# When the second quarter of w_in, the second stage's matrix and the first conversion come in a spectral MLP kernel's start

## The chip, the cores and the metric

The kernel runs on one core of a Trainium2 chip. The metric is the device time of one execution in microseconds (us), the median of several executions. TensorE (PE) multiplies matrices, with weight loads shown apart as PEld; VectorE (DVE) and ScalarE (ACT) do element-wise work; SyncE (SP) and ScalarE issue the DMA transfers that matter here.

## The reference

The input x is (8, 3008, 256). Each batch goes through a real FFT along its 3008 rows, a complex linear map with a soft threshold, and an inverse FFT; the rows that come out go through a two-layer network with a leaky ReLU. Cut to what is computed:

```python
X = np.fft.rfft(x, axis=1)
Yr = Xr @ w_r - Xi @ w_i + b_r
Yi = Xr @ w_i + Xi @ w_r + b_i
Yr = np.sign(Yr) * np.maximum(np.abs(Yr) - 0.01, 0.0)   # Yi alike
y = np.fft.irfft(Y, n=3008, axis=1)
h = y @ w_in                       # 256 -> 2048
out = np.maximum(0.01 * h, h) @ w_out   # 2048 -> 256
```

w_in and w_out arrive as 64-bit floats, which the kernel reads as pairs of 32-bit words and converts itself.

## The kernel before, in words

3008 is 47 x 64, so each FFT is done in two stages of small matrix products. For one batch b:

- `fwd(b)` is the first stage (47 points). It loads x in seven column chunks of two halves (L237 for batch 0), forms sums and differences of the halves on DVE (`fold`, L247 and L248), multiplies each of the 14 results by a matrix in fa (`stage_a`, L264; the bank tag `psh` has four buffers), copies the product back to SBUF on ACT (L266) and stores it to `u_dram` (L269, issued on SP for batch 0). The list `turned` holds the copy, `written` the stores.
- `mid(b)` is the second stage (64 points) with the linear map. For each of 12 pairs j of frequencies it reads `u_dram` back with two loads in another order (L331, kept in `reads`, three `u` buffers), multiplies by slices of fb (`stage_b`, L345), evicts on ACT (L349) and DVE (L350), multiplies by the weights (`proj`, L80), adds the bias (L382), thresholds (L390 to L392), scales (L396, L400), and multiplies by gb (`stage_g`). The result is copied (L418) and stored to `v_dram` by ACT (L420). Pair j uses index 0 of fb and the two indices 2j+1 and 2j+2, out of 25.
- `inverse` and `forms` do the last 47-point stage and make token chunks of 512 columns; `moe` runs the two-layer network on 47 such chunks (L94 for w_in, L609 for w_out).

Turning the first spectrum means that all 14 stores of batch 0 have to land before the first read of `mid(0)`, since the reads cut across every chunk.

Around this the start of the program does the constants. `load_win(c)` loads quarter c of w_in in two transfers of 512 KB each (L157); quarters 0 and 1 share a buffer tile, as do 2 and 3. `convert_win(c)` turns it from 64-bit floats into a high and a low 32-bit part: two operations on ACT (L133, L134), five on DVE (L135 to L139), one sum (L164), four small combinations (L167 to L170) and three splits (L173 on ACT, L174 on DVE). `split_consts` does the same splitting for the other constants (L114 on ACT, L115 on DVE).

The order of work on each engine is set by a planner that simulates the program (`schedule_with_timeline_sim=True`, L867). The code steers it with `tc.issue_after(ins)`: what is traced inside such a block is put behind `ins` on the engine of `ins`, and left free on the other engines. Data dependences come on top by themselves. Before the change these were the hints at the start: the second quarter's loads on SP behind the eighth store (`written[7]`), `convert_win(0)` without a hint, `split_consts` and `convert_win(1)` on ACT behind the last of the 14 copies (`turned` held only the last), the bias, quarters 2 and 3 and ga on SP behind the fourth read (`reads[3]`).

The main loop alternates `moe_a`, `moe_b` and `moe_o` of successive chunks on PE in a fixed order, with the spectra of later batches laid in between.

Of the kernel before, what the change touches and what calls it, by code (L numbers as in the profile page):

```python
# [8 lines left out]
F32 = mybir.dt.float32  # L9
# [9 lines left out]
N1, N2, NK1 = 47, 64, 24  # L19
NG, NS = 5, 13  # L20
P = 128
# [9 lines left out]
def spectral_mlp_kernel(  # L31
# [33 lines left out]
    const = ctx.enter_context(tc.tile_pool(name="const", bufs=1))  # L65
# [3 lines left out]
    sync, act, dve, pool = nc.sync, nc.scalar, nc.vector, nc.gpsimd  # L69

    def bank(tag, bufs):
        return ps.tile([P, 512], F32, name=tag, tag=tag, bufs=bufs)

    def products(dst, pairs):

        terms = []
        for l, r in pairs:
            terms += [(l[0], r[0]), (l[0], r[1]), (l[1], r[0])] if len(l) == 2 else [(l[0], r[0])]
        for i, (a, b) in enumerate(terms):
            last = nc.tensor.matmul(dst, a, b, start=(i == 0), stop=(i == len(terms) - 1))  # L80
        return last
# [18 lines left out]
    consts = {}  # L100

    def pair(name, shape):
        consts[name] = tuple(const.tile(shape, F32R, name=f"{name}_{p}") for p in ("hi", "lo"))
        return consts[name]

    def load_plain(name, src, shape):
        consts[name] = const.tile(shape, F32, name=name)
        sync.dma_start(consts[name], src)
# [19 lines left out]
    def float64_parts(raw, a, q):  # L128


        wl, wh = raw[:, :, 0], raw[:, :, 1]
        u = a.bitcast(U32)
        act.mul(q, wl, 2.0 ** -52)  # L133
        act.activation(a, wh.bitcast(F32), AF.Abs, scale=2.0 ** 16)  # L134
        dve.tensor_scalar(a, a, F64_MIN * 2.0 ** 16, F64_MAX * 2.0 ** 16, ALU.max, ALU.min)  # L135
        dve.tensor_scalar(u, u, 4, 1, ALU.logical_shift_left, ALU.logical_shift_right)
        dve.scalar_tensor_tensor(u, wh, 0x80000000, u, ALU.bitwise_and, ALU.bitwise_or)
        dve.tensor_scalar(wl, u, 0xFF800000, None, ALU.bitwise_and)
        dve.tensor_mul(q, q, wl.bitcast(F32))  # L139
# [8 lines left out]
    def load_win(c, queues, behind=None):  # L148
        if c % 2 == 0:
            tag = ("wout_hi", "wout_lo")[c // 2]  # L150
            raw = sb.tile([P, 2, NH * NIN, 2], U32, name="win_raw", tag=tag, bufs=1)
            win_raw.extend((raw[:, 0], raw[:, 1]))
        r = win_raw[c].rearrange("p (a f) w -> p a (f w)", a=NH)
        iv = w_in.bitcast(U32).rearrange("(a p) f -> p a f", p=P)[:, :, 2 * c * NIN:2 * (c + 1) * NIN]
        for a, q in enumerate(queues):
            with tc.issue_after(behind.ins) if behind is not None else nullcontext():
                q.dma_start(r[:, a], iv[:, a])  # L157

    def convert_win(c):


        a, q, s = win_tmp
        float64_parts(win_raw[c], a, q)
        dve.tensor_add(a, a, q)  # L164
        a = a.rearrange("p (j q i m) -> p j q i m", j=NH, q=2, i=2)
        a11, a12, a21, a22 = (a[:, j, :, i] for i in range(2) for j in range(2))
        dve.tensor_add(s[:, 0], a21, a22)  # L167
        dve.tensor_sub(s[:, 2], a11, a21)
        dve.tensor_sub(s[:, 1], s[:, 0], a11)
        dve.tensor_sub(s[:, 3], a12, s[:, 1])  # L170
        hi, lo = (w[:, :, 2 * c:2 * c + 2] for w in consts["win"])
        for k, w in ((slice(0, 2), a[:, :, :, 0]), (2, a22), (slice(3, 7), s)):
            act.copy(hi[:, k], w)  # L173
            last = dve.tensor_sub(lo[:, k], w, hi[:, k].bitcast(F32))  # L174
        return last
# [37 lines left out]
    reads, written, turned, turning, thresholded = [], [], [], [], []  # L213
# [4 lines left out]
    def fwd(b):  # L218
        ud = dram.tile([2, NK1, NG * NS, D], F32, name="u_dram", tag="u_dram", bufs=NPRE + 1)
        u_dram[b] = ud  # L220
        uv = ud.rearrange("c k (g s) d -> c (k g) (s d)", g=NG)
        x_t, s_t = {}, {}

        def load(c):
            cols = slice(2 * c * D, min(2 * c + 2, NS) * D)
            n = cols.stop - cols.start
            if b < NPRE:
                tag, bufs = (XT, XT1)[b][c]
                x2 = sb.tile([PA, 2, 2 * D], F32, name="xin", tag=tag, bufs=bufs)
                x_t[c] = [x2[:, h, :n] for h in range(2)]  # L230
            else:
                x_t[c] = [
                    sb.tile([PA, 2 * D], F32, name=f"xin{h}", tag="uv"[h], bufs=3 - h)[:, :n] for h in range(2)
                ]
            for h, t in enumerate(x_t[c]):
                if b == 0:
                    (act if h else sync).dma_start(t, x[b, h, :, cols])  # L237
                else:
                    with tc.issue_after(reads[-1].ins):
                        sync.dma_start(t, x[b, h, :, cols])  # L240

        def fold(c):
            xa, xb = x_t[c]
            n = xa.shape[1]
            eng = dve
            xs = sb.tile([PA, 2 * D], F32, name="xs", tag="zf", bufs=1)[:, :n] if b else xs3[:, c % 3, :n]
            eng.tensor_add(xs, xa, xb)  # L247
            eng.tensor_sub(xa, xa, xb)  # L248
            s_t[c] = [(xs,), (xa,)] if b < NPRE else [xs, xa]

        def split(c, h):
            t = s_t[c][h]
            n = t.shape[1]
            z = sb.tile([PA, 2, 2 * D], F32R, name="xz", tag="ez"[h], bufs=1)
            xh, xl = z[:, 0, :n], z[:, 1, :n]
            dve.tensor_copy(xh, t)
            dve.tensor_sub(xl, t, xh.bitcast(F32))  # L257
            s_t[c][h] = (xh, xl)

        def stage_a(c, h):  # L260
            t = x_t[c][h]
            n = t.shape[1]
            pa = (bank("psf", 2) if b else bank("psh", 4))[:PA, :n]
            products(pa, [(consts[f"fa{h}"] if b else consts[f"fa{h}32"], s_t[c][h])])  # L264
            t = x_t[c][1 - h]
            cp = act.copy(t, pa)  # L266
            if b == 0:
                turned[:] = [cp]
            st = (act if b else sync).dma_start(uv[h, :, 2 * c * D:2 * c * D + n], t)  # L269
            if b == 0:  # L270
                written.append(st)

        def stage_a1(c):

            n = x_t[c][0].shape[1]
            pas = [(bank("psf", 2) if c in (4, 5) else bank("psh", 4))[:PA, :n] for _ in range(2)]
            for h in range(2):
                with tc.issue_after(turning[NPAIR - 2].ins):
                    products(pas[h], [
                        (consts[f"fa{h}32"], (x_t[c][0],)), (consts[f"fa{2 * h}32"], (x_t[c][1],))])  # L280
            for h in range(2):
                act.copy(x_t[c][h], pas[h])
                sync.dma_start(uv[h, :, 2 * c * D:2 * c * D + n], x_t[c][h])

        if b == 1:
            for c in range(NX):
                load(c)
                yield 0
            for c in (0, 1, 2, 3, 6, 4, 5):
                stage_a1(c)  # L290
                yield 6 * x_t[c][0].shape[1]
            return

        ahead = 2 if b >= NPRE else NX
        for c in range(ahead):
            load(c)
        yield 4 * CS if b >= NPRE else 0
        fold(0)
        if b >= NPRE:
            split(0, 0)  # L300
        yield 0
        for c in range(NX):
            for h in range(2):
                if h == 0 and c + ahead < NX:
                    load(c + ahead)
                if h == 0 and c + 1 < NX:
                    fold(c + 1)
                stage_a(c, h)
                if b >= NPRE and (c + h < NX):
                    split(c + h, 1 - h)  # L310
                yield 3 * x_t[c][h].shape[1]
# [381 lines left out]
    f0 = Stream(fwd(0), FWD)  # L693
    f0.to(0.01)
    load_win(0, (sync, act))
    load_plain("fb", fb, [P, NK1 + 1, N2])
    load_weights()
    sign = const.tile([P, NK1 + NPAIR], F32, name="sign")
    sync.dma_start(sign, sg)
    sync.dma_start(consts["gb32"][0], gb)  # L700
    f0.finish()
    load_win(1, (sync, sync), written[7])
    pair("win", [P, 7, NQ, P])
    win_tmp = (
        sb.tile([P, NH * NIN], F32, name="cva", tag="vin"), sb.tile([P, NH * NIN], F32, name="cvq", tag="gf"),
        sb.tile([P, 4, 2, P], F32, name="ws", tag="yh"))
    act.mul(fa32[:, 2], fa32[:, 1], -1.0)
    convert_win(0)
    with tc.issue_after(turned[0].ins):
        split_consts()  # L710
    m0 = Stream(mid(0), MID)
    m0.to(0.001)
    bias = const.tile([P, 2, D], F32, name="bias")
    with tc.issue_after(reads[3].ins):
        for r, src in enumerate((b_r, b_i)):
# [3 lines left out]
    with tc.issue_after(reads[3].ins):  # L719
        load_plain("ga", ga, [PA, 2, P])  # L720
    fp = Stream(fwd(1), FWD)
    with tc.issue_after(turned[0].ins):
        convert_win(1)
    wout = load_wout()
    for i in range(1, 17):
# [147 lines left out]
```

## Time and profile before

| | us |
|---|---|
| median of 3 runs | 2574.14 |
| the three runs | 2566.14, 2574.14, 2575.76 |
| the profiled execution | 2568.88 |
| its span, from first to last instruction | 2567.10 |
| PE busy in the span | 2527.2 (98%) |
| DVE busy | 1882.8 (73%) |
| ACT busy | 1677.5 (65%) |

The profiled execution took 1.78 us more than its span. It lies between the shortest and the other two runs. In the timeline, each row gives the start in us, the time in us, the engine, the line in the kernel, the operation, what it writes and reads and how many instructions are merged in the row; in brackets stands how long the engine was idle before, and what it waited for. SPq and ACTq rows are the issuing of DMA transfers, not the transfers themselves. In the table by stages, the columns are the length of the stage, the busy us of each engine with its instructions in brackets, the granted TensorE clock (1 is full speed), the busy share of the 16 DMA engines, and the GB/s that they moved.

### The profile page before, as it was taken

The numbers are of one execution on the slowest core, as the hardware profiler recorded it, in microseconds if no ns is written. First come the engines' busy times: TensorE is split into PE (matmuls) and PEld (weight loads), VectorE is DVE, ScalarE is ACT, GpSimd is POOL, SyncE is SP. The second block draws the span as 40 slices with busy tenths as digits, with TensorE's granted clock in tenths as the row PEclk, the third lists the DMA queues.
The fourth block names the chain that finished last, engine by engine and source line by source line (L and its number), as shares of the span: only waits on it lengthen the run. The fifth ranks groups of instructions, "written<-read, shape, count | busy, mean of one in ns | idle before, by whom it ended". The sixth has DMA issues, their size and how long they took to land.

```text
span 2567.1 us, 42449 instructions
## 1 busy us (share of the span) xinstructions
PE 2527.2 (98%) x16204; PEld 2269.8 (88%) x16204; DVE 1882.8 (73%) x3460; ACT 1677.5 (65%) x3151; POOL 118.9 (5%) x96
## 2 busy tenths in 40 slices
PE   6999999999999999999999999999999999999999
PEld 4689888999899998999989999899998998999998
DVE  7787777777877778777787677867768777666665
ACT  4776666677566765677666676567665676655564
POOL 0001000000000000000000000000000000000000
PEclk8999999999999999999999999999999999999999
DMA  8631133111321113111141111412114111100000
GB/s 267 176 93 50 42 91 88 41 50 45 103 67 46 50 37 112 59 49 49 42 113 53 50 49 38 120 54 58 34 38 132 46 54 41 44 21 29 9 17 17
DMA packets 119904, 165.12 MB, mean 64 GB/s; under 512 B 13597, under 2 KB 69909, under 8 KB 119701
## 3 DMA queue, kind: packets, MB, share of 16 engines
q1 hardware_dynamic: 79112, 115.54, 14.7%
q10 hardware_dynamic: 40589, 46.87, 7.1%
q8 instruction: 128, 2.10, 0.4%
q14 instruction: 75, 0.61, 0.1%
HBM read 86.60 MB, written 75.76 MB: 63 GB/s over the span
## 4 chain that ended last, share of the span: by engine, by line
PE 89%; DMA 4%; DVE 3%; ACT 2%; issue 1%; ACTq 0%; SPq 0%; DVEq 0%
PE pso L609 38%; PE psh L94 34%; PE psf L80 11%; PE psf L482 3%; PE psf L345 3%; DMA xin<-x_dram 1%; DMA u_dram<-xin 1%; PE psh L80 1%; DVE gl L562 1%; DMA v_dram<-v 0%; DMA u<-u_dram 0%; DVE xz L257 0%; DVE gf L593 0%; ACT zf L400 0%; DMA vin<-v_dram 0%
## 5 line engine op out<-in xcount | busy, mean ns | idle before, releaser
L94 PE MATMUL psh<-yh,win_hi 128*128 128x256 f32 (+1 forms) x2608 | 741.3, 285 | 2.1 <-DVE gf L593 2.0
L94 PE MATMUL psh<-yl,win_hi 128*128 128x256 f32 (+1 forms) x2608 | 732.3, 281 | 0.0
L94 PE MATMUL psh<-yh,win_lo 128*128 128x256 f32 (+1 forms) x2608 | 729.6, 281 | 0.0
L562 DVE TENSOR_TENSOR gl<-gf,gh 128x1024 fp32r<-128x1024 f32 x376 | 461.0, 1226 | 309.8 <-ACT gh L560 305.9
L609 PE MATMUL pso<-gl,wout_hi 128*128 128x512 f32 x1504 | 591.6, 393 | 1.1 <-DVE gl L562 1.1
L609 PE MATMUL pso<-gh,wout_hi 128*128 128x512 f32 x1504 | 591.1, 393 | 1.0 <-ACT gh L560 1.0
L609 PE MATMUL pso<-gh,wout_lo 128*128 128x512 f32 x1504 | 589.6, 392 | 0.0
L94 PEld LDWEIGHTS psh<-yh,win_hi 128*128 128x128 f32 x2608 | 489.9, 188 | 19.7 <-DVE gf L593 4.9
L94 PEld LDWEIGHTS psh<-yl,win_hi 128*128 128x128 f32 x2608 | 490.4, 188 | 17.4 <-issue 0.5
L94 PEld LDWEIGHTS psh<-yh,win_lo 128*128 128x128 f32 x2608 | 489.0, 188 | 2.1
L560 ACT CAST gh<-gf 128x1024 fp32r<-128x1024 f32 x376 | 395.3, 1051 | 44.4 <-PE pso L609 34.9
L596 ACT ACTIVATE gf<-gf 128x768 f32<-128x768 f32 x368 | 311.7, 847 | 150.4 <-DVE gf L593 139.4
L609 PEld LDWEIGHTS pso<-gl,wout_hi 128*128 128x128 f32 x1504 | 282.5, 188 | 61.4 <-DVE gl L562 2.9
L609 PEld LDWEIGHTS pso<-gh,wout_hi 128*128 128x128 f32 x1504 | 282.8, 188 | 47.3 <-ACT gh L560 1.8
L609 PEld LDWEIGHTS pso<-gh,wout_lo 128*128 128x128 f32 x1504 | 282.5, 188 | 46.5 <-issue 0.2
L595 ACT ACTIVATE gf<-psh 128x256 f32<-128x256 f32 x368 | 142.0, 386 | 239.1 <-PE psh L94 232.0
L593 DVE TENSOR_TENSOR gf<-psh,u 128x512 f32<-128x512 f32 x368 | 252.4, 686 | 34.4 <-PE psh L94 30.7
L577 ACT COPY p<-psh 128x256 f32<-128x256 f32 x368 | 137.0, 372 | 158.0 <-PE psh L94 149.6
L382 POOL TENSOR_TENSOR kb<-bias,kc 128x512 f32<-128x512 f32 x84 | 116.3, 1385 | 2074.3 <-ACT kc L380 1877.0
L578 DVE TENSOR_TENSOR u<-psh,p 128x256 f32<-128x256 f32 x368 | 154.6, 420 | 73.8 <-ACT p L577 72.6
L580 DVE TENSOR_TENSOR gf<-psh,u 128x256 f32<-128x256 f32 x368 | 154.8, 421 | 31.1 <-PE psh L94 17.2
L581 DVE TENSOR_TENSOR gf<-psh,gf 128x256 f32<-128x256 f32 x368 | 154.5, 420 | 5.5
(128 smaller groups left out, 3173.0 us busy)
## 6 DMA issues: line engine op xcount, KB each, us to landing
u<-u_dram SPq DMA_DIRECT2D x192, 128.0 KB, 2.8
v_dram<-v ACTq DMA_DIRECT2D x192, 128.0 KB, 2.4
out_dram<-ob SPq DMA_DIRECT2D x94, 256.0 KB, 2.0
vin<-v_dram SPq DMA_DIRECT2D x96, 240.0 KB, 3.6
xin<-x_dram SPq DMA_DIRECT2D x90, 240.0 KB, 3.0
u_dram<-xin ACTq DMA_DIRECT2D x72, 240.0 KB, 2.4
u_dram<-xin SPq DMA_DIRECT2D x24, 240.0 KB, 4.4
raw<-w_out_dram SPq DMA_DIRECT2D x8, 512.0 KB, 5.3
```

What stands on the lines that cost most here:

```text
L80: last = nc.tensor.matmul(dst, a, b, start=(i == 0), stop=(i == len(terms) - 1))
L94: mlp[:] = [nc.tensor.matmul(dst, a, b, start=start and i == 0, stop=i == 2, skip_group_check=True)]
L560: cp = act.copy(gh, g)
L562: parted[:] = [cp, dve.tensor_sub(gl, g, gh.bitcast(F32))]
L577: act.copy(p1, b1[:, lo])
L578: dve.tensor_add(u2, b1[:, hi], p1)
L580: dve.tensor_add(g[:, 3], b2[:, hi], u2)
L581: dve.tensor_add(g[:, 3], b2[:, lo], g[:, 3])
L593: dve.tensor_add(g[:, 1:3], b2.rearrange("p (k n) -> p k n", k=2), u2.unsqueeze(1).broadcast_to([P, 2, HT]))
L595: act.activation(g[:, 0], b1[:, lo], AF.Prelu, alpha=SLOPE)
L596: act.activation(g[:, 1:4], g[:, 1:4], AF.Prelu, alpha=SLOPE)
L609: mlp[:] = [nc.tensor.matmul(po, a[:, f, s], r[:, i], start=(f == 0 and j == 0), stop=(f == NF - 1 and j == 2),)]
```

## The change

Five edits at the start of the program; nothing is computed otherwise.

1. `turned` now keeps all 14 copies of the first stage of batch 0, so `turned[9]` is the tenth and `turned[-1]` the last.
2. `convert_win(0)` is put on ACT behind the tenth copy.
3. `split_consts` and `convert_win(1)` stay behind the last copy, which is now written `turned[-1]`.
4. The second quarter of w_in (two transfers of 512 KB, on SP) goes from behind the eighth store to behind the fourth read, ahead of the bias.
5. fb (800 KB) is loaded in two parts: indices 0 to 6 where it stood, indices 7 to 24 behind the fourth read and the second quarter of w_in.

```diff
@@ -265,7 +265,7 @@
             cp = act.copy(t, pa)
             if b == 0:
-                turned[:] = [cp]
+                turned.append(cp)
@@ -693,23 +693,27 @@
     load_win(0, (sync, act))
-    load_plain("fb", fb, [P, NK1 + 1, N2])
+    consts["fb"] = const.tile([P, NK1 + 1, N2], F32, name="fb")
+    sync.dma_start(consts["fb"][:, :7], fb[:, :7])
     load_weights()
...
     f0.finish()
-    load_win(1, (sync, sync), written[7])
     pair("win", [P, 7, NQ, P])
...
     act.mul(fa32[:, 2], fa32[:, 1], -1.0)
-    convert_win(0)
-    with tc.issue_after(turned[0].ins):
+    with tc.issue_after(turned[9].ins):
+        convert_win(0)
+    with tc.issue_after(turned[-1].ins):
         split_consts()
     m0 = Stream(mid(0), MID)
     m0.to(0.001)
+    load_win(1, (sync, sync), reads[3])
+    with tc.issue_after(reads[3].ins):
+        sync.dma_start(consts["fb"][:, 7:], fb[:, 7:])
     bias = const.tile([P, 2, D], F32, name="bias")
...
     fp = Stream(fwd(1), FWD)
-    with tc.issue_after(turned[0].ins):
+    with tc.issue_after(turned[-1].ins):
         convert_win(1)
```

## The prediction

> **What bounds the kernel now.** First the table by stages (columns: stage, its length, busy us of PE, PEld, DVE, ACT, POOL, granted clock, DMA share, GB/s):
>
> ```profile
> 0.00:20.00 20.00, 10.68 (x20) 4.11 (x20) 8.98 (x14) 6.35 (x10) 0.77 (x6) 1.00 0.91 281
> 20.00:31.60 11.60, 5.48 (x8) 2.41 (x8) 8.66 (x14) 6.39 (x15) 0.00 (x0) 0.51 1.02 366
> 31.60:36.00 4.40, 0.53 (x2) 0.56 (x3) 3.25 (x8) 2.37 (x4) 0.00 (x0) 0.50 0.60 188
> 36.00:50.00 14.00, 12.86 (x61) 11.61 (x60) 13.06 (x23) 6.50 (x10) 0.00 (x0) 0.83 0.88 249
> 50.00:64.00 14.00, 11.67 (x62) 9.24 (x61) 13.93 (x23) 8.55 (x17) 0.00 (x0) 1.00 0.71 213
> 64.00:100.00 36.00, 31.35 (x141) 23.42 (x142) 25.68 (x46) 29.18 (x57) 0.00 (x0) 1.00 0.56 150
> 100.00:120.00 20.00, 19.55 (x72) 10.91 (x71) 16.81 (x31) 12.34 (x25) 0.00 (x0) 1.00 0.82 246
> 120.00:2567.10 2447.10, 2435.07 (x15844) 2207.56 (x15843) 1792.38 (x3306) 1605.87 (x3018) 118.18 (x90) 1.00 0.20 56
> ```
>
> From 120 us on PE works 2435.07 of 2447.10 us: **PE is the bound**, and its idle time there is 12.0 us in all. An edit that takes no work off PE can therefore only bring the main loop's start, at 120 us, forward or put it back. Ahead of that the bound changes: DMA is full up to 31.6 us (share 0.91, then 1.02), DVE is full from 36 to 64 us (13.06 and 13.93 of 14), and PE and ACT share the rest.
>
> Next the timeline of the stage that the change touches: ACT first, then PE, SP and the first operations behind the turn.
>
> ```profile
> 13.05 2.54 ACT L266 COPY xin<-psh 120x512 f32<-120x512 f32 x5 [1.70 <-PE psh L80]
> 18.27 1.12 ACT L133 ACTIVATE cvq<-win_raw 128x1024 f32<-128x1024 uint32 x1 [2.67 <-DMA win_raw<-w_in_dram]
> 19.28 1.12 ACT L134 ACTIVATE cva<-win_raw 128x1024 f32<-128x1024 f32 x1
> 20.28 2.06 ACT L266 COPY xin<-psh 120x512 f32<-120x512 f32 x4
> ...
> 26.44 0.37 ACT L266 COPY xin<-psh 120x256 f32<-120x256 f32 x1 [0.48 <-PE psh L80]
> ```
>
> ```profile
> 16.36 1.02 PE L80 MATMUL psh<-xs,fa 120*120 120x512 f32 x2
> 17.22 1.02 PE L80 MATMUL psh<-xin,fa 120*120 120x512 f32 x2
> 20.93 2.06 PE L80 MATMUL psh<-xs,fa 120*120 120x512 f32 x2 [2.68 <-ACT xin L266]
> ...
> 25.34 1.06 PE L80 MATMUL psh<-xin,fa 120*120 120x256 f32 x2
> ```
>
> ```profile
> 23.10 0.67 SPq L157 DMA_DIRECT2D win_raw<-w_in_dram  x1
> 23.86 4.81 SPq L269 DMA_DIRECT2D u_dram<-xin  x6
> 28.73 0.42 SPq L157 DMA_DIRECT2D win_raw<-w_in_dram  x1
> 31.57 3.95 SPq L331 DMA_DIRECT2D u<-u_dram  x6
> ```
>
> ```profile
> 35.47 5.46 PE L345 MATMUL psh<-fb,u 128*128 128x128 f32 x24 [9.06 <-DMA u<-u_dram]
> ```
>
> ACT had made six of the 14 copies when it came to the first conversion (L133) and stood for its load, 2.67 us. With four `psh` buffers PE then had nowhere to write and stood too (2.68 us), and its granted clock fell to 0.51. The last copy ends at 26.81 us, the reads that need all stores go out at 31.57, and the second stage starts at 35.47. Up to the stores two things run side by side: the chain of copies, and a full DMA system in which the second quarter of w_in and all of fb travel with the stores.
>
> **The change part by part.** *First conversion behind the tenth copy.* Nothing is added; two ACT operations change places with four copies. The tenth product starts at 17.22 and ends at 18.24, its copy ends near 18.24 + 0.59 = 18.83. L133 and L134 then take 20.40 - 18.27 = 2.13 us (the second ends at 20.40), to 20.96. Meanwhile PE does products 11 to 14: 0.86 us apart at full clock (17.22 - 16.36), half of that for the last two, so all are done by 20.7. Four copies follow: 2 x 0.515 (2.06 / 4) + 2 x 0.37 = 1.77 us, and the last ends at 22.73 instead of 26.81: 4.08 us earlier. If the clock drops all the same, PE needs the 5.49 us that it needed (from 20.93 to 26.42) from 18.08 on, and the last copy ends at 23.94: 2.87 earlier. I take 4.08, since the gap that preceded the low clock is the one removed. The Trainium skill, page "TensorE: Matmul & The Clock Gate", section "What's actually happening", has the clock fall after an idle window of about 3.4 us; here 2.68 us of idle stood before it. By that rule too the full clock would stay, so the sum would be the same 4.08.
>
> DVE waits for L134 at its L135 0.56 us longer (20.96 against 20.40), with the later operations of that conversion and the constants' splits queued behind; these splits wait for ACT's work behind the last copy, which comes 4 us earlier, so this costs nothing.
>
> *Second quarter and fb behind the reads.* The transfers:
>
> ```profile
> fb<-fb_dram SPq DMA_DIRECT2D x1, 800.0 KB, 5.1
> win_raw<-w_in_dram SPq DMA_DIRECT2D x7, 512.0 KB, 6.7
> ```
>
> 18 of 25 indices of fb are 576 KB; with 2 x 512 KB that is 1.64 MB out of the stretch ahead of the reads. The second of the two, issued at 28.73, was partly behind it anyway: if it landed after 6.7 us, 3.9 of them lay behind 31.57, 0.30 MB. So 1.34 MB leave, at 366 GB/s 3.7 us. The copies allow 4.08, DMA 3.7: the reads go out **3.7 us earlier**, near 27.9 (2.87 is the lower bound, 4.08 the upper).
>
> *What comes next.* The same 1.34 MB now stands on SP's queue behind six reads, ahead of the bias, quarters 2 and 3, ga and the reads of pairs 3 to 5:
>
> ```profile
> 35.57 0.60 SPq L716 DMA_DIRECT2D bias<-b_r_dram  x1
> 36.21 0.42 SPq L716 DMA_DIRECT2D bias<-b_i_dram  x1
> 36.68 2.69 SPq L157 DMA_DIRECT2D win_raw<-w_in_dram  x4
> 39.41 0.87 SPq L108 DMA_DIRECT2D ga<-ga_dram  x1
> 40.38 6.33 SPq L331 DMA_DIRECT2D u<-u_dram  x6
> ```
>
> ```profile
> 49.84 1.13 PE L345 MATMUL psh<-fb,u 128*128 128x128 f32 x8 [1.14 <-DMA u<-u_dram]
> ```
>
> PE waits for pair 3 at 49.84, so that read is on the path, and what stands in front of it counts. The moved loads cost it 3.7 us if nothing is idle, and less as they fill idle DMA time: 0.40 x 4.4 = 1.76 us behind the reads, and 0.12 x 14 = 1.68 us from 36 to 50. Given back: between 3.7 - 3.44 = 0.3 and 3.7 us. I take the first gap alone as filled, because the moved loads are issued right there, and the second lies behind them: 1.9 us given back, 1.8 kept. The one extra DMA issue on SP, at most the 0.60 us of the bias row, is hidden while SP's transfers queue up. The fb indices that pairs 0 to 2 use (up to 6) arrive first; pair 3 is the first to need the rest, which stands ahead of its own read.
>
> *DVE.* From 36 to 64 us it is idle for 1.01 us only, so a gain passes only if its work starts earlier too. The second conversion starts there at:
>
> ```profile
> 37.57 0.57 ACT L349 COPY ef<-psh 128x512 f32<-128x512 f32 x1
> 37.70 0.69 DVE L135 TENSOR_SCALAR cva<-cva 128x1024 f32<-128x1024 f32 x1 [0.84 <-ACT cva L134]
> ```
>
> Its load would now be issued near 27.9 + 3.95 = 31.9 and land 6.7 later, near 38.6; with 2.1 us on ACT, DVE gets it near 40.7, 3 us late, while the second stage's own DVE work comes 3.7 us early and can fill that. These about cancel, and 1.8 us stays the term.
>
> *Sum.* From 64 us on nothing is changed, and PE (31.35 of 36, 19.55 of 20) and ACT carry the shift on: 2568.88 - 1.8 = 2567.1 for the profiled execution. This lies 5.3 below the median of 2574.14, and the runs shown spread over 9.6 us, more than the change. The mean of all four (2566.14, 2568.88, 2574.14, 2575.76) is 2571.2, so the forecast is **2569.4 us**. A measurement of this kernel can tell about 0.5%, 12.9 us, from no change.
>
> **The rivals.** *All is kept.* The moved loads fill all the idle DMA time, and DVE follows: -3.7, 2567.5. For it speaks the low 188 GB/s behind the reads; against it the full DVE.
>
> *Nothing is left.* The bytes are only moved, the read of pair 3 lands when it did, and DVE ends its stretch when it did: 2571.2. For it speaks the wait at 49.84, against it the idle share of 0.40 behind the reads. The Trainium skill, page "DMA: Bandwidth & Descriptors", section "Issuing engines are not separate DMA queues", says that all issuers share the same 16 engines; the share of 1.02 up to 31.6 us agrees, and by it alone this rival is the outcome.
>
> *Slower.* The planner keeps L133 and L134 of the second conversion ahead of the first L349 on ACT, as they stand now (L349 at 37.57 follows them directly). The load lands near 39.1 (its second half issued 0.5 us later), ACT is done with both at 41.2, and the first eviction of the second stage comes at 41.2 instead of 37.57, with PE, DVE and all later pairs behind it: +3.6, 2574.8; with a landing 1.3 us later 2576. It decides from the point where the load lands after 35.5, when L133 started before. Against it: the planner simulates the load too, and may put L133 behind.
>
> *The main loop is ordered otherwise.* The planner sees other times, and PE's 12.0 us of idle time change: up to twice as much, 2583, or half as much, 2565.
>
> **How the numbers follow.** Chances: forecast 0.45 (gain 0.8 to 2.8, 2568.4 to 2570.4), all kept 0.15, nothing left 0.20, slower 0.15, main loop 0.05. Three of five lie within 2567.5 to 2571.2, and a median of few runs can lie 5 us off the mean as the shown one's runs do (2566.14 and 2575.76). That gives 2562 to 2577. Faster by over 0.5% (below 2561.3) needs all kept and a low draw of runs: 0.05. Slower by over 0.5% (above 2587.0) needs more than the main-loop case's price or a slower case dearer than worked out: 0.04. Within: 0.91.
>
> **What would show it.** Right: ten copies (L266) ahead of L133 on ACT, no PE wait on ACT between 17 and 21 us, the last copy near 22.7, the first L331 near 27.9, the first L345 near 31.8, the main loop's first L94 about 2 us earlier. The give-back shows in the start of pair 3's L345: about 48 rather than 49.84 or 46. Wrong: an L133 ahead of the first L349 with ACT idle for win_raw in front; a DVE idle time over 3 us between 36 and 64; or PE idle times behind 120 us that differ from 12.0 us by more than the 1.8 forecast.

## The result, and the profile after

The changed kernel is **slower by 0.18%**: 2574.27 us (median of 12 runs, 2572.61 to 2575.94) against 2569.63 us (median of 12 runs of before, 2566.14 to 2575.76), a ratio of 1.0018 with a 95% interval of 1.0010 to 1.0025. The prediction had 1.8 us less; there are 4.6 us more. Within 0.5% it still is, as the largest chance had it, but the interval excludes no change, and on the other side.

The profiled execution took 2573.71 us, near the median. In the table by stages of after (columns as before: length, PE, PEld, DVE, ACT, POOL, granted clock, DMA share, GB/s):

```profile
20.00:31.60 11.60, 1.41 (x6) 0.68 (x4) 10.10 (x17) 6.07 (x14) 0.00 (x0) 0.73 0.80 289
31.60:36.00 4.40, 3.08 (x14) 3.11 (x15) 1.83 (x5) 1.00 (x3) 0.00 (x0) 0.50 0.72 196
36.00:50.00 14.00, 11.07 (x48) 8.90 (x46) 8.59 (x15) 4.51 (x7) 0.00 (x0) 0.90 0.94 302
50.00:64.00 14.00, 12.16 (x54) 9.44 (x55) 10.76 (x21) 9.86 (x20) 0.00 (x0) 0.88 0.73 206
120.00:2571.90 2451.90, 2439.78 (x15874) 2212.62 (x15872) 1795.24 (x3311) 1609.45 (x3025) 118.16 (x90) 1.00 0.20 57
```

The last row first: PE's idle time behind 120 us is 2451.90 - 2439.78 = 12.1 us, before 12.0. **The main loop has not changed; the loss is ahead of it.** The first L94 stands at 124.70 us, before at 120.17: 4.5 of the 4.8 us by which the span grew.

```profile
123.76 1.17 PE L482 MATMUL psf<-ga,vin 120*128 120x128 f32 x9
124.70 0.73 PE L94 MATMUL psh<-yh,win_hi 128*128 128x512 f32 x2
```

Now DVE. Before it worked 13.06 of the 14 us from 36 to 50 and 13.93 of the next 14; after it is 8.59 and 10.76. From 36 to 64 us it does 19.35 us of work where it did 26.99: 7.6 us are lost there. The turn itself came earlier, as the timelines of ACT, SP and PE show:

```profile
18.86 0.59 ACT L266 COPY xin<-psh 120x512 f32<-120x512 f32 x1 [0.27 <-PE psh L80]
19.35 1.14 ACT L133 ACTIVATE cvq<-win_raw 128x1024 f32<-128x1024 uint32 x1
20.38 1.12 ACT L134 ACTIVATE cva<-win_raw 128x1024 f32<-128x1024 f32 x1
21.39 1.61 ACT L266 COPY xin<-psh 120x512 f32<-120x512 f32 x4
```

```profile
29.24 4.02 SPq L331 DMA_DIRECT2D u<-u_dram  x6
33.30 1.07 SPq L157 DMA_DIRECT2D win_raw<-w_in_dram  x2
34.41 0.42 SPq L716 DMA_DIRECT2D fb<-fb_dram  x1
34.88 0.60 SPq L720 DMA_DIRECT2D bias<-b_r_dram  x1
```

```profile
32.92 5.72 PE L345 MATMUL psh<-fb,u 128*128 128x128 f32 x24 [11.52 <-DMA u<-u_dram]
...
51.79 1.42 PE L345 MATMUL psh<-fb,u 128*128 128x128 f32 x8 [3.74 <-DMA u<-u_dram]
```

Ten copies stand ahead of L133, the last of the 14 ends at 23.00 (26.81 before), the reads go out at 29.24 (31.57), the second stage starts at 32.92 (35.47). And behind that, on ACT and DVE:

```profile
40.30 1.15 ACT L133 ACTIVATE cvq<-win_raw 128x1024 f32<-128x1024 uint32 x1 [3.01 <-DMA win_raw<-w_in_dram]
```

```profile
37.71 0.42 DVE L350 TENSOR_TENSOR ef<-ef 128x256 f32<-128x256 f32 x1
42.51 0.69 DVE L135 TENSOR_SCALAR cva<-cva 128x1024 f32<-128x1024 f32 x1 [4.38 <-ACT cva L134]
43.71 0.69 DVE L382 TENSOR_TENSOR kb<-bias,pso 128x512 f32<-128x512 f32 x1 [0.51 <-DMA bias<-b_i_dram]
```

The second conversion's L135 starts at 42.51 (37.70 before), with 4.38 us of idle time in front. Behind it in DVE's queue stands the bias sum of the first pair, and that waits for the bias as well. The third conversion's L135 comes at 65.67, 13.7 us later than before (51.98):

```profile
65.67 0.69 DVE L135 TENSOR_SCALAR cva<-cva 128x1024 f32<-128x1024 f32 x1
```

So nearly all of a conversion, 9.7 us of DVE work (the sum of its rows), now lies behind 64 us, where before only the last 2.8 us of it did; DVE has the second stage to do there as well. The table for 64 to 82 us, first before, then after:

```profile
64.00:82.00 18.00, 16.04 (x78) 12.80 (x79) 13.62 (x24) 15.43 (x29) 0.00 (x0) 1.00 0.86 241
```

```profile
64.00:82.00 18.00, 15.54 (x79) 12.00 (x78) 17.84 (x32) 12.84 (x25) 0.00 (x0) 1.00 0.91 264
```

DVE is full (17.84 of 18) where it had 4 us of air. PE's starts of a pair show what that does: pair 7 starts at 69.05, even earlier than before (69.78), and pairs 9, 10 and 11 start at 80.59, 84.93 and 89.56 against 78.62, 82.96 and 86.93. Two waits of PE stand between pairs 7 and 9, of 1.13 and 1.19 us. The trace puts them down to a load of x and a store of v, but each ends where ScalarE's last scaling of what the product reads ends (L400, at 73.77 and 79.57). What had held ScalarE up, DVE or its own issuing of stores, these rows do not settle. Of the 4.53 us by which the first L94 is late, 2.63 are there at pair 11; the other 1.90 come behind it, in a stretch where the granted clock is low (0.53 from 100 to 106 us, 1.00 before). That makes a theory, and three rivals for it.

### The profile page after: what moved, and what is told of

The parts are those of the page before. It is cut to its first block, busy times and chain, and to the rows that moved or that the text cites. A ratio compares the mean times of both kernels' runs of the same rounds, so it can differ in the third digit from the quotient of the medians.

```text
span 2571.9 us, 42454 instructions
## 1 busy us (share of the span) xinstructions
PE 2530.1 (98%) x16204; PEld 2271.8 (88%) x16204; DVE 1883.0 (73%) x3460; ACT 1677.8 (65%) x3151; POOL 118.9 (5%) x96
## 4 chain that ended last, share of the span: by engine, by line
PE 93%; DMA 3%; DVE 1%; ACT 1%; issue 1%; SPq 0%; ACTq 0%; DVEq 0%
PE pso L609 39%; PE psh L94 35%; PE psf L80 11%; PE psf L482 3%; PE psf L345 3%; PE psh L80 1%; DMA xin<-x_dram 1%; DMA u<-u_dram 1%; DMA fb<-fb_dram 0%; DVE gl L562 0%; DMA v_dram<-v 0%; DMA win_raw<-w_in_dram 0%; ACT zf L400 0%; DMA u_dram<-xin 0%; PE psh L345 0%
## 5 line engine op out<-in xcount | busy, mean ns | idle before, releaser
L94 PE MATMUL psh<-yh,win_hi 128*128 128x256 f32 (+1 forms) x2608 | 740.9, 285 | 1.9 <-DVE gf L593 1.9
L94 PE MATMUL psh<-yl,win_hi 128*128 128x256 f32 (+1 forms) x2608 | 732.4, 281 | 0.0
L94 PE MATMUL psh<-yh,win_lo 128*128 128x256 f32 (+1 forms) x2608 | 729.6, 281 | 0.0
L94 PEld LDWEIGHTS psh<-yl,win_hi 128*128 128x128 f32 x2608 | 490.4, 188 | 17.9 <-issue 0.5
L94 PEld LDWEIGHTS psh<-yh,win_hi 128*128 128x128 f32 x2608 | 489.9, 188 | 18.5 <-DVE gf L593 3.6
L94 PEld LDWEIGHTS psh<-yh,win_lo 128*128 128x128 f32 x2608 | 489.1, 188 | 2.1
L580 DVE TENSOR_TENSOR gf<-psh,u 128x256 f32<-128x256 f32 x368 | 154.8, 421 | 31.6 <-PE psh L94 17.4
```

The lines of the kernel that those rows point to most:

```text
L94: mlp[:] = [nc.tensor.matmul(dst, a, b, start=start and i == 0, stop=i == 2, skip_group_check=True)]
L580: dve.tensor_add(g[:, 3], b2[:, hi], u2)
```

## The experiments

The theories, by the letters of the expectations:

- **F**, DVE's backlog: the second quarter of w_in lands too late to feed DVE behind the turn, and the work that DVE does not do there makes it the limit later.
- **C** is its first half alone: the wait for the second conversion.
- **D**, the queue: 1.6 MB more stand ahead of the read of pair 3, and that read is the limit.
- **E**, the clock: the last pairs end with waits on PE, its clock drops, and the work behind takes longer.

Each kernel was timed in five rounds beside before, and ratios are to before in the same rounds. Medians of different rounds differ by up to 1 us for before itself (2569.38 to 2570.18), and most intervals here are 0.18% wide, some 4.6 us. The planner orders each kernel anew, so an edit also moves work that it does not name. All edits are of before or of the full change; line numbers in the profiles of the experiments differ from before's by a few.

### The tie alone

```diff
-    convert_win(0)
+    with tc.issue_after(turned[9].ins):
+        convert_win(0)
```

> Before plus one edit: the first conversion on ScalarE behind the tenth copy; the second quarter of w_in and fb stay where they were. Theory D (queue): what the full change loses, it loses because 1.6 MB more stand on SP's queue ahead of the read of pair 3, which went from 49.84 to 51.79 us. Then this edit keeps a gain: reads about 2 us earlier (near 29.5), pair 3's first L345 at 48 to 49, main loop's first L94 1 to 2 us before 120.17, total 1 to 2 us under before. Theory C (conversion): the loss comes from the second quarter's late load, for which DVE stood 4.38 us at its L135. Here that load is early, so the same gain is expected. Theory E (end of the second stage): the loss comes from how the last pairs end and from the low TensorE clock behind them; then this can come out on either side, by as much as the clock near 100 us says.

Measured: 1.0014 (1.0005 to 1.0023), slower. The profiled execution, at 2568.78 us the fastest of its 11 runs, has the last copy at 23.1, yet the reads later than before. SP's timeline in the kernel with the tie alone:

```profile
23.74 0.62 SPq L157 DMA_DIRECT2D win_raw<-w_in_dram  x1
24.46 0.64 SPq L269 DMA_DIRECT2D u_dram<-xin  x1
25.15 0.41 SPq L157 DMA_DIRECT2D win_raw<-w_in_dram  x1
25.65 2.84 SPq L269 DMA_DIRECT2D u_dram<-xin  x5
34.00 1.35 SPq L331 DMA_DIRECT2D u<-u_dram  x2
```

With the copies earlier, the planner put the second load of the quarter ahead of the last five stores; before, it was behind all of them. The reads went out at 34.00 instead of 31.57. None of the theories had expected this: moving copies forward gained nothing for the reads, since the quarter's bytes now went ahead of five stores. Since the traced run was the fastest of its 11, the trace shows the order and not the loss. The second conversion was not late here: its L135 started at 36.86 (37.70 before).

### The tie with one of the two moves

The first kernel leaves out the split of fb, the second leaves the second quarter's loads where they were (behind the eighth store).

> The full change without the split of fb: all 800 KB of fb travel ahead of the stores, the second quarter behind the reads. Theory D: 1.05 MB instead of 1.64 MB moved, so pair 3's L345 comes about 1.3 us earlier than in the full change, near 50.5, if the reads go out no later; they go out about 1.5 us later, which takes it back. Total 3 to 5 us over before. Theory C: the second quarter is as late as in the full change, DVE stands 3 to 5 us at L135, total 4 to 5 us over before. Theory E: follows the clock near 100 us.

> The full change without moving the second quarter: it travels among the stores as before; 0.59 MB of fb go behind the reads. Theory D: 0.59 MB more ahead of pair 3's read is 1.6 us at 366 GB/s, against reads some 2 to 3 us earlier: pair 3's L345 at 48 to 49.5, total 0 to 2 us under before. Theory C: no wait of DVE for the second conversion (under 1 us), total 1 to 2 us under before. Theory E: follows the clock near 100 us.

Measured: 1.0016 (1.0007 to 1.0025) and 1.0011 (1.0003 to 1.0020). The first came out as C and D have it (pair 3 at 50.71, DVE standing 3.94 us at its L135). In the second, both loads stand among the stores as with the tie alone, and the reads go out at 34.35. D's and C's gains for it did not come. As with the tie alone, the second conversion came early (L135 at 36.20): a late second conversion is one way to lose, and late reads are another.

### The full change with the fourth quarter late

```diff
-    for c in range(2, 4):
-        load_win(c, (sync, sync), reads[3])
+    load_win(2, (sync, sync), reads[3])
...
         m0.to(i / 16)
+        if i == 5:
+            load_win(3, (sync, sync), reads[-1])
```

> The full change, and the fourth quarter of w_in (1.05 MB, first used near 102 us) behind a later read, so that it stands on SP's queue behind the reads of pairs 3 to 6. Theory D: pair 3's L345 comes 2 to 3 us earlier than 51.79, near 49, and the total 2 to 3 us under the full change's 2574.3. Theory C: the second conversion is as late as in the full change (DVE waits 4 us at L135), so the total stays at 2573 to 2575 even though pair 3's read lands earlier. Theory E: follows the clock near 100 us.

Measured: 1.0019 (1.0010 to 1.0028). The read of pair 3 landed earlier (its L345 at 48.95, before even before's 49.84), and the total did not move. **D falls here for the first time**: the read was late in the full change, but it was not what the time hung on.

### The bias first

The two bias loads go ahead of `load_win(1)`; the rest is the full change.

> The full change with the two bias loads put ahead of the second quarter and the rest of fb on SP's queue. Theory F (DVE's backlog): the full change loses because DVE stands idle behind the turn (10.02 busy of 18 us from 32 to 50, before 15.91), since both things it could do there, the bias sum L382 and the second conversion L135, wait for loads that land at 43.7 and 40.3; what it did not do then makes it full from 64 to 82 us (17.84 of 18), and pairs 8 to 11 and all behind them come late. With the bias there by 39 or 40 DVE starts L382 there, is busy 12 us or more of the 18, and the total falls 1.5 to 3 us below the full change's, to 2571 to 2573. Theory D (queue): the same bytes stand ahead of pair 3's read, so its L345 stays at 51 to 52 and the total at 2574 (within 1 us). Theory E (end of the second stage): the total goes by the clock between 100 and 106 us.

Measured: 1.0016 (1.0007 to 1.0025), 2573.24 us. That is above the 2571 to 2573 of F, within the 1 us of D, and not clear of the full change. DVE's busy time from 32 to 50 us is 9.05 us, not 12 or more as F had it: the bias sum now starts at 41.58, but the second quarter lands later behind the bias, and its L135 starts at 45.88. Of the two late loads only one was exchanged for the other. From 64 to 82 us DVE is busy for 14.91 of 18 us here, and the loss is the same: a full DVE in that stretch is what after shows, and not a condition of the loss.

### The second quarter between the stores and the reads

```diff
-    load_win(1, (sync, sync), reads[3])
+    load_win(1, (sync, sync), written[13])
```

> The full change with the second quarter behind the last store and ahead of the first read, so that it moves while the stores land. Theory F: it lands by 34 to 36, the second conversion's L135 starts at 36 to 39 without a wait over 1 us, DVE is busy 14 us or more from 32 to 50, and the total falls to 2568 to 2571, no worse than before. Theory D: 0.6 MB more than before stand between the reads and pair 3, pair 3's L345 near 48 to 50, total 2570 to 2572. Theory E: the total goes by the clock between 100 and 106 us, on either side.

Measured: 1.0009 (1.0000 to 1.0018), 2570.07 us against 2569.38 for before in the same rounds and 2573.24 for the kernel with the bias first. By the ratio half of the loss is back, by the medians most of it. PE and DVE in this kernel:

```profile
36.47 4.47 PE L345 MATMUL psh<-fb,u 128*128 128x128 f32 x24 [15.37 <-DMA u<-u_dram]
```

```profile
38.62 0.69 DVE L135 TENSOR_SCALAR cva<-cva 128x1024 f32<-128x1024 f32 x1
```

The second stage starts at 36.47, **3.5 us later** than in the full change and 1 us later than before, since the quarter's 1 MB is ahead of its reads in the queue. The conversion starts at 38.62 instead of 42.51, and the total is lower. Between these two kernels, when the second stage starts is not what counts; that DVE gets the second conversion earlier goes with the lower total. F's figure of 14 us of DVE work from 32 to 50 was too high (12.63), its total was right. D's total (2570 to 2572) was right as well, with pair 3 at 50.10, so this kernel alone does not part the two.

### One conversion left out, on before and on the full change

```diff
-            convert_win(2)
+            for w in consts["win"]:
+                pool.tensor_copy(w[:, :, 4:6], w[:, :, 2:4].bitcast(F32))
```

> Before, with the third quarter of w_in not converted: GpSimd copies the second quarter's converted parts in its place, which takes some 9.7 us of DVE work (L135 to L174 of one conversion) and 4.4 us of ACT work out of the stretch from 45 to 75 us. It is the partner of the next kernel. Theory F: the total falls by 1 to 4 us. Theories D and E: by under 1 us, since the loads and the end of the stage stay.

> The full change with the same conversion left out. Theory F: with 9.7 us of DVE work gone the backlog is worked off by 70 us, DVE is under 14 of 18 us from 64 to 82, and the difference to the same cut of before is under 1.5 us instead of 4. Theory D: pair 3's read is as late as in the full change and the difference of the two stays at 3 to 5 us. Theory E: the difference stays unless the clock between 100 and 106 us goes up to 1.

Measured: 1.0007 (0.9997 to 1.0016) and 1.0004 (0.9995 to 1.0013). In the shortened before nothing is gained, against F's 1 to 4 us; in the shortened full change **no loss is left that can be measured**. The change costs 0.18% with that conversion; without it, it is 0.04% over before and 0.03% under the shortened before. The table and the timeline of the shortened full change:

```profile
64.00:82.00 18.00, 17.80 (x92) 14.33 (x92) 13.09 (x21) 13.62 (x29) 3.75 (x2) 1.00 0.91 266
```

```profile
120.21 0.71 PE L94 MATMUL psh<-yh,win_hi 128*128 128x512 f32 x2
```

DVE has air again (13.09 of 18), PE is full (17.80), and the first L94 stands at 120.21, where before has it. All this with pair 3 as late as in the full change, at 51.94. It is the second blow to D, and the most direct support for F: the late load costs only while that conversion's work is there. What it does not part is DVE's share from ACT's, since ACT loses 4.3 us of the same conversion; that DVE was full there and ACT was not (12.84 of 18) speaks for DVE, but from 32 to 82 us both did less in after than before (DVE 38.63 us against 43.46, ACT 28.21 against 32.84). Nor does it rule out E: the clock from 100 to 106 us is 0.88 here, in after 0.53.

### The tie, with the stores undisturbed

The tie on before, and the second quarter's loads behind `written[13]`; fb is one load.

> Before, with the first conversion on ScalarE behind the tenth copy, and the second quarter's loads behind the last store and ahead of the reads; fb in one load as before. In the kernel with the tie alone the planner put both loads of the quarter ahead of the last five stores, and the reads went out at 34.00 instead of 31.57. Theory S (stores): that is what the tie alone costs; here the stores go first, the reads go out near 30 to 31, and the total is 2568 to 2570.5, equal to before within 0.1%. Theory F (DVE's backlog): DVE is over 13 us busy from 32 to 50 and L135 of the second conversion starts by 40; total as before. If the total stays 3 us or more over before, neither load order nor DVE's backlog is what the tie costs.

Measured: 1.0001 (0.9992 to 1.0010). The loss of the tie alone is not there, which fits the order of loads and stores as its cause; the intervals of the two kernels overlap. Reads at 31.09, L135 at 38.79, DVE 14.30 of 18 us from 32 to 50.

### Four more products to hold the clock

```diff
+                if j in (9, 10):
+                    for _ in range(2):
+                        nc.tensor.matmul(bank("pso", 2), consts["gb32"][0], flat(z_last[0]), start=True, stop=True)
```

> The full change with four more matrix products (128x512, never read) on TensorE, two each behind the second stage's tenth and eleventh last product, where PE waits in the full change (2.21 and 1.22 us) and its granted clock then falls to 0.53 from 100 to 106 us. Theory E (clock): the clock stays at 0.9 or more there, the last product and the 24 products of batch 1 behind it take 1.1 and 10.5 us instead of 2.07 and 11.86, and the total falls by about 2 us, to 2572. Theory F says that this is a part of the loss only: at least 2 us over before remain. If the clock stays up and the total does not fall, the low clock there was not on the path.

The table of after for 100 to 106 us, and of this kernel:

```profile
100.00:106.00 6.00, 4.78 (x6) 1.48 (x6) 3.43 (x6) 2.83 (x6) 0.00 (x0) 0.53 0.37 87
```

```profile
100.00:106.00 6.00, 5.53 (x13) 2.08 (x12) 5.78 (x9) 3.24 (x8) 0.00 (x0) 1.00 0.32 75
```

The clock stayed up. Measured: 1.0014 (1.0005 to 1.0023), 2573.01 us, some 1 us under the full change, and the intervals overlap. E had 2 us. The traces show that this is no clean test of E: from pair 11's L345 to the first L94 this kernel takes 32.80 us (91.10 to 123.90), after 35.14 and before 33.24, so what E expected came behind pair 11; but pair 11 itself came 1.5 us later than in after. How much of the loss is E's stays open; the 2.63 us that after is late at pair 11 lie ahead of that stretch. The Trainium skill, page "TensorE: Matmul & The Clock Gate", section "What's actually happening", has the clock of an idle TensorE halve after a window of about 3.4 us. The 0.53 agrees with that half; the idle times do not agree with that window, since the clock fell in after behind 2.21 and 1.22 us, and in before (0.54 from 20 to 24 us) behind 2.68.

### Can the early turn be had without the loss?

Two kernels put the second quarter between stores and reads, the bias ahead of the rest of fb, and the fourth quarter (in the second one the third too) behind later reads.

> The full change with three moves: the second quarter behind the last store and ahead of the reads, the bias ahead of the rest of fb, and the fourth quarter behind the reads of pairs 3 to 6. Theory F: DVE is over 13 us busy from 32 to 50 and nothing is lost; pair 3's read has 1 MB less ahead of it (its L345 near 47 to 49), so first L94 at 118 to 121 and a total of 2566 to 2570, at or under before. Theory D gives the same or 1 us less. If it is 2571 or more, something else than these loads costs.

> The kernel before this one in the list, with the third quarter as well behind the reads of pair 3, so that only the bias, the rest of fb and ga stand ahead of them. Theory D: pair 3's L345 comes at 43 to 46, and the total is 2 to 4 us lower than with the third quarter ahead (2564 to 2567). Theory F: the third quarter's conversion has slack (it started near 52 us in before), PE and DVE are full from 64 us on anyway, and the total stays within 1.5 us of the kernel before it in the list.

Measured: 1.0002 (0.9993 to 1.0011) and 1.0001 (0.9992 to 1.0010). Neither is faster than before. Both run without a loss that can be measured, and with them the kernels sort by one thing: the five kernels that compute all with the second quarter behind the reads (the full change, no split of fb, the fourth quarter late, the bias first, four more products) stand at 1.0014 to 1.0019, and the four so far with it between the last store and the reads at 1.0001 to 1.0009. In the second, pair 3 starts 2.8 us earlier than before, and pair 4 later:

```profile
47.06 1.05 PE L345 MATMUL psh<-fb,u 128*128 128x128 f32 x8
...
55.74 1.05 PE L345 MATMUL psh<-fb,u 128*128 128x128 f32 x8
```

```profile
50.00:64.00 14.00, 11.74 (x58) 8.75 (x57) 13.81 (x26) 11.11 (x20) 0.00 (x0) 1.00 0.99 266
```

DVE is full again (13.81 of 14). Would less work on DVE let the early reads through? Three more kernels: the second one with the third quarter's conversion left out as above; with the sums, products and differences of that conversion on GpSimd (`eng = pool if c in (2,) else dve`), which computes all; and the same on the tie with undisturbed stores.

> best2 (second quarter ahead of the reads, bias ahead of the rest of fb, third and fourth quarter behind later reads) with the third quarter not converted: GpSimd copies the second quarter's parts in its place. Theory F (DVE is the limit from 36 to 82 us): with 9.7 us of DVE work gone, pair 4's L345 comes at 51 to 53 instead of 55.74, the first L94 at 116 to 119 instead of 122.29, and the total falls by 2 to 4 us, under before's. Theory G (a limit behind 64 us, TensorE's own pace of 4.34 us for a pair, or the loads of batch 1): the total stays within 1 us of best2 and before.

> best2 with the sums, products and differences of the third quarter's conversion on GpSimd (ten instructions, 6.4 us on DVE, about twice that on GpSimd by the 1.39 us of its 128x512 sum against 0.69 on DVE); all is computed. Theory F: 6.4 us less on DVE, the total falls by 1 to 3 us, to 2567 to 2569. Theory G: within 1 us of before. If GpSimd's steps hold up ScalarE's castings of that quarter, which queue ahead of the second stage's copies, it is slower than best2.

> tie_w13 (before with the first conversion behind the tenth copy and the second quarter between the last store and the reads) with the same part of the third quarter's conversion on GpSimd; all is computed. Theory F: 1 to 3 us under before. Theory G: within 1 us of before.

Measured: 1.0000 (0.9991 to 1.0009), 1.0006 (0.9998 to 1.0015) and 1.0002 (0.9993 to 1.0010). F's gains did not come. In the first kernel the chain of waits goes through a load that ACT waited for (ACT itself was idle for the last 2.83 us of it):

```profile
50.11 6.57 DMA win_raw<-w_in_dram
56.73 0.04 issue
56.77 1.17 ACT cvq L133
```

The fourth quarter's first operation had come ahead of the second stage's work in ACT's queue and waited for its load: the same trap once more. From 64 to 82 us PE was then full (18.00 of 18). What keeps all these kernels at before's time is not settled. TensorE's own pace from 64 us on is the candidate (18.00 of 18 in the shortened before and in the shortened best2), argued from the tables and not shown by an experiment. Where the first L94 stands does not settle it either: in the last kernel it stands at 124.88, as late as in after, and the time is 1.0002. No kernel here beats before.

## Why the prediction was wrong, point by point

- **What bounds the kernel, and the first conversion behind the tenth copy: right.** PE's 12.0 us of idle time in the main loop stayed (12.1). The last copy came at 23.00 against a forecast of 22.73, and PE's wait on ACT between 17 and 21 us was gone; the last products ran at full clock (1.00 from 20.0 to 21.8 us).
- **The reads 3.7 us earlier: mis-sized.** They came 2.33 us earlier, under the lower bound of 2.87. The bytes left as forecast: up to where the reads go out, before moved 9.87 MB (by 31.6 us) and after 8.49 MB (by 29.3 us; rates times lengths of the stages), 1.38 MB less against a forecast of 1.34. What the sum left out is the rate at both ends. Up to 20 us after moved 264 GB/s where before moved 281, some 0.9 us at 366 GB/s, and while the last stores landed, from 28.0 to 29.3 us, it moved 199 GB/s, another 0.6 us.
- **What is given back at pair 3: mis-sized and, worse, not on the path.** Forecast 1.9 us of 3.7; pair 3 came 1.95 us late, so of 2.33 us earlier reads 4.28 were given back. The queue ahead of it took more than the full-rate bound of 3.7. But the fourth quarter late moved pair 3 to 48.95 and left the total, the full change with the conversion left out kept pair 3 at 51.94 and lost nothing, and best2 had it at 47.06 and gained nothing. "That read is on the path" was a reading of one wait, and did not hold: PE made up the delay by pair 7.
- **The step that failed is DVE's: "These about cancel, and 1.8 us stays the term."** The late conversion was foreseen (L135 "near 40.7, 3 us late"; it was 4.8 late), and that the second stage's own DVE work would fill the gap was assumed. It could not: its first large piece, the bias sum, needs the bias, which the same move had put behind 1.6 MB, and DVE's queue had L135 ahead of it. DVE did 7.6 us less work between 36 and 64 us, where the prediction's own table had shown 1.01 us of idle time to spare. A stretch in which an engine is full has no room for a late start; that is the price that was set to nothing. That the late quarter costs is shown by where it stands (1.0014 to 1.0019 behind the reads, 1.0001 to 1.0009 ahead of them), and that it costs by way of the conversions' work by the shortened pair of kernels. How the 4.6 us divide among DVE, ACT and the low clock behind the last pairs is not shown.
- **The rival "slower"** had the right load and the wrong victim. It expected ACT to hold up the first eviction of the second stage behind L133. The planner put L133 behind two evictions, as the rival's counter-argument said; the wait hit DVE, and on ACT only the third eviction (42.38 us) stood behind it. The landing did come after its point of decision of 35.5. That its price of 3.6 us lies near the measured 4.6 is luck, since the path was another.
- **The rivals "all is kept" and "nothing is left"** fell with the total. The sentence of the Trainium skill on the shared 16 engines (page "DMA: Bandwidth & Descriptors", section "Issuing engines are not separate DMA queues") agreed with the traces as far as it goes: bytes moved behind the reads were paid there, with pair 3 1.95 us later. That the total then stays, as the rival had it, did not follow: DVE stood for the moved bytes meanwhile (4.38 us at L135).
- **Spread of runs.** The three runs shown first (median 2574.14) lay high; the median of 12 was 2569.63. The forecast stood on the mean of four, 2571.2, and was 1.6 us too high for before. As a time it missed by 4.9 us, as a difference by 6.4; that the miss in time is the smaller one is luck of the first draw.

## What to carry to other kernels

Before a load is moved behind something, look at which engine its data feeds, and how much idle time that engine has in the stretch where the data used to arrive: if there is next to none, the delay can come back later, whatever starts earlier in exchange. And a single wait on the path does not make it the limit; check whether the engine catches up some rows further down. A hint that moves one instruction also lets a planner reorder what is not tied: here the tie of one conversion put a bulk load ahead of five stores.

## What the runs showed that was not expected

- A second stage that starts 3.5 us later (36.47 against 32.92) goes with a total that is lower, 1.0009 against 1.0018.
- Leaving out 9.7 us of DVE work and 4.3 us of ACT work changes before by nothing that can be measured (0.9997 to 1.0016), and brings the full change to 1.0004 (0.9995 to 1.0013).
- A GpSimd sum takes about twice DVE's time here (2.67 us against 1.22 us for 128x1024), and moving nine sums, products and differences of one conversion to a GpSimd that was otherwise idle there gained nothing.
